# A new hand-written order of steps: the first loads move between two issuing queues, and a weight's last rows are loaded later

## The chip, the cores and the metric

The kernel runs on one core of one Trainium2 chip. The metric is device time in microseconds of one execution. Times are medians of several runs; the profile is of one further execution.

## The reference

One token sequence x of 2048 rows by 448 columns is normalised once, and the result feeds two branches, whose outputs are added to x.

```python
xn  = layernorm(x)                                  # over the 448 columns
q, k, v = split_heads(xn @ wqkv)                    # 16 heads of 28
phi(t) = concat(softmax(t @ w_phi), softmax(-(t @ w_phi)))      # per head, 56 features
kv  = einsum("sf,sd->fd", phi(k), v);  z = phi(k).sum(s)
o   = (phi(q) @ kv) / (phi(q) @ z + 1e-6)
h   = xn @ w1 + b1                                  # 1792 columns
out = x + o @ wo + (h * tanh(softplus(h))) @ w2
```

All tensors are bfloat16.

## The kernel before, in words

The 2048 rows lie as 16 tiles of 128 rows; two tiles make a *pair* u (tiles 2u and 2u+1), eight pairs in all. The program is a list of named steps. A string, `ORDER` (line 147), names them one after the other; `run_order` calls each, and a step appends its instructions to the queues of the engines that do it. Every engine (PE, DVE, ACT, POOL) and SP, which only issues transfers, then works through its own queue in that order. Waits between engines are derived from what a step reads and writes. So the string sets, for each engine, what stands behind what; a step that waits holds up all that follows on its engine. ACT issues a few transfers too, from the same queue as its arithmetic.

The steps that matter here:

- `lx1`, `lx2`, `lx3` load one pair of x each (line 270; "first pair" in the order of use is pair 3, tiles 6 and 7), `lx6`, `lx0`, `lx4` the rest. The last letter is the issuer: s for SP, a for ACT. `lp` loads w_phi (298), `lb` the bias (302).
- `lkm`, `lvm` load rows 0 to 383 of the K and V columns of wqkv into Wk and Wv (273); `lkt` loads the last 64 rows of both, twice, into the two halves of the partitions (281, the *tails*). `l1m0` to `l1m2` and `l1t` do the same for W1 (277, 281). `lqT0` to `lqT3` load the transposed Q columns (285). `l2s`, `los` load W2 and Wo.
- `z12` is twelve warm-up products of constants on PE. `wtk0` to `wtk3` transpose Wk on PE (556), `wmk`, `wmq` multiply Wk and WqT by the block-diagonal phi matrix that POOL builds (`bd`, 544); this folds phi into the projections Wpk and Wpq. Of these names the last letter is the engine that copies the result out of PSUM (a: ACT, d: DVE).
- Per pair: `st` statistics of a tile (467), `rs` the inverse deviation (on ACT or POOL), `xn` the normalised tiles (501 on DVE, 496 on POOL), `xt` the transpose into xnT: on PE with a copy (509; a, d, or b for half on ACT and half on DVE), or by a transfer (m, 521).
- `v`, `k`, `q` with a pair's number and part 1 or 2 are the projections of that pair (438; eight and six products). ACT takes the exponents of k and q; `kn` divides by their sums (608 to 612); `e` followed by a tile's number transposes a tile's exponents of q by a transfer (669).
- `f` is the first layer of the second branch with W1 (438, with 512 columns), `kv` sums phi(k) times v (629), `nd` is the attention's quotient (703 to 729), `wo`, `G`, `g` are the output products (805 to 843), and `sto` the stores.

Each part of six products waits for the end of its part of eight, and results leave PSUM through four pairs of banks. The transposing transfers of xn and of the exponents, the plain loads and SP's waits all share SP's one queue.

Of the kernel before, what the change touches and what calls it, by code (L numbers as in the profile page):

```python
# [144 lines left out]


ORDER = """
lpa pp2 lx3s pm z12 st6d pi lkms table st7d pw lx1a lkts lba lvma bd rs3t wtk2a xn3d lx2s lqT2 wtk0d st3d pv wtk1a wmk2a
xt3a wtk3d lqT1 wmk0a wmk1a st2d wmk3a st5d v31d rs1p lqT0 st4d xn1d rs2p lqT3 b1 qd lx6s v32a k31 lx0s wmq1a lx4s pp1
wmq0a xn2p l1ts xt1d st14d st15d wmq2a wmq3a k32 k11 st12d rs7p st9d q11 xt2m st8d k12 st10d xn7d q31 rs4p v11d pp0 q12  # L150
xn4p st11d v12d q21 rs5p st13d q32 q22 xn5p k21 st0d l1m2s l1m0s rs6p xt7m v21d k22 st1d v22a ep e3 rs0p v71a pk xt4m
k71 v72a kn3.1 xn6d k72 xt5m k41 xn0d kn3.0 e2 xt6m xt0m v41d e5 k42 l1m1s v42d e4 q41 v51d q42 e6 e8 v52a kn2.0 k61
v61d k62 kn4.0 k01 k51 kn7.0 kn4.1 k02 v62d q51 k52 q52 kn0.0 e7 q61 e9 v01d q62 e12 kn1.1 kn6.1 e10 f0.11 e11 kn1.0
v02d f0.12 kn0.1 f1.01 f0.21 f1.02 f1.21 kn7.1 f1.31 f1.22 los kn2.1 q71 f1.32 f1.51 kn5.0 f0.22 e13 f1.52 q01 q72 q02
f0.61 l2s kn6.0 kv3 kv1 e15 kv2 kn5.1 kv4 kv6 e14 kv7 kv0 kv5 kvz f0.62 f0.71 f0.91 f1.81 f0.72 e1 f1.82 f0.121 f1.111
f0.122 f0.81 f0.92 f1.112 f0.82 f1.91 f0.131 f1.92 e0 nd2 f0.132 f0.31 f0.101 f0.32 nd0 f0.111 f0.102 f0.112 nd1 f1.71
f1.61 f1.72 f0.51 nd3 f1.62 f0.52 f1.41 f1.11 f0.01 f1.12 f0.41 f1.42 ot0m nd5 f0.42 f0.02 wo01 f1.131 f1.101 ot1m nd6
f1.132 G01 nd4 f1.102 G11 ot2m wob nd7 ot3m G02 wo02 f1.121 nd12 G12 f1.122 wo11 nd11 wo22 G31 wo31 nd10 wo12 G21 nd13
ot5m ot6m wo21 wo32 G62 nd8 G22 wo52 G32 nd9 ot4m wo61 G51 nd15 G61 nd14 wo51 G41 wo62 sto6 sto1 wo41 G52 ot7m g14 sto5
wo7F sto2 G42 wo7H sto0 wo42 g15 stt14 sto3 sto4 stt15  # L160
"""


# [824 lines left out]
```

## Time and profile before

| | us |
|---|---|
| runs before the change | 150.36, 150.85, 152.3; median 150.85 |
| the profiled execution | 150.35, of which the span is 148.3 |
| PE busy | 143.7 (97% of the span) |
| DVE, ACT, POOL busy | 100.7, 72.0, 44.4 |
| granted PE clock | 0.999 |

The span runs from the first instruction to the last. A row of the timeline gives the start, the time from the first instruction of a group to the end of the last, the engine, the line and operation, what is written from what is read, and how many instructions are merged; behind it, in brackets, how long the engine was idle before and what ended that. SPq and ACTq rows are the issuing of transfers, not their flight. A row of the windows view gives the stretch and its length, then the busy time and count of instructions of PE, PE's weight loads, DVE, ACT and POOL, then the granted clock, the mean busy share of the 16 DMA engines, and GB/s. A row on DMA issues ends with the KB of each transfer and the median time from issue to landing.

### The profile page before, as it was taken

How to read it: one execution, taken by the hardware profiler on the slowest of the kernel's cores; microseconds unless marked ns; L12 is line 12 of the kernel's file. 1: busy time of each engine (PE TensorE's matmuls, PEld its weight loads, DVE VectorE, ACT ScalarE, POOL GpSimd, SP SyncE). 2: the span in 40 equal slices, each digit the busy share in tenths (PEclk: the TensorE clock that was granted, in tenths of full speed). 3: DMA queues.
4: the chain of work that ended last, by engine and by line, in shares of the span. 5: the costliest groups of instructions: out<-in, count | busy, mean ns of one | idle time of the engine just before them, and what ended most of it. 6: DMA issues, size and time to landing. Idle time of an engine off the chain costs nothing.

```text
span 148.3 us, 3988 instructions
## 1 busy us (share of the span) xinstructions
PE 143.7 (97%) x1731; PEld 75.9 (51%) x1731; DVE 100.7 (68%) x225; ACT 72.0 (49%) x83; POOL 44.4 (30%) x65
## 2 busy tenths in 40 slices
PE   7799999999999999999999999999999999999993
PEld 2456456556555475444454445555555555554452
DVE  0888889897999803003998278896789859983042
ACT  3589889978996899578566653202000000000000
POOL 5428489899899990000000000000000000000000
PEclk9999999999999999999999999999999999999999
DMA  5999998999939989960003300031003300306513
GB/s 123 301 190 346 182 275 130 163 205 256 139 67 174 242 242 267 210 113 0 0 4 62 62 4 0 21 73 34 4 2 66 62 0 4 62 4 186 186 52 134
DMA packets 39997, 17.24 MB, mean 116 GB/s; under 512 B 33964, under 2 KB 39212, under 8 KB 39980
## 3 DMA queue, kind: packets, MB, share of 16 engines
q1 hardware_dynamic: 38800, 16.29, 52.5%
q10 hardware_dynamic: 1180, 0.70, 1.9%
q8 instruction: 13, 0.21, 0.6%
q14 instruction: 4, 0.03, 0.1%
HBM read 7.02 MB, written 1.84 MB: 60 GB/s over the span
## 4 chain that ended last, share of the span: by engine, by line
PE 89%; DMA 6%; DVE 2%; issue 0%; ACT 0%; SPq 0%
PE PS L438 47%; PE PS L843 31%; PE PS L805 3%; DMA Wkv<-in_A_wqkv_dram 3%; DMA xnT<-xn 3%; PE PS L703 2%; PE PS L629 2%; PE PS L571 1%; PE PS L821 1%; DVE stats L467 1%; PE PS L556 1%; PE PS L509 1%; DVE xnT L516 0%; ACT Eq L514 0%; DVE x_all L770 0%
## 5 line engine op out<-in xcount | busy, mean ns | idle before, releaser
L438 PE MATMUL PS<-xnT,W 64*128 64x512 bf16 x392 | 44.8, 376 | 0.0
L680 ACT ACTIVATE actT<-PS,b1T 128x1024 bf16<-128x1024 f32 x28 | 30.1, 1112 | 24.3 <-PE PS L438 24.3
L843 PE MATMUL PS<-W,actT 64*128 64x448 bf16 x392 | 39.3, 349 | 0.0
L438 PEld LDWEIGHTS PS<-xnT,W 64*128 64x128 bf16 x392 | 18.8, 94 | 20.8 <-ACT actT L680 0.5
L843 PEld LDWEIGHTS PS<-W,actT 64*128 64x128 bf16 x392 | 18.1, 94 | 18.1 <-issue 0.3
L612 POOL TENSOR_TENSOR actT<-actT,rSk 128x896 bf16<-128x896 bf16 x16 | 26.6, 1702 | 0.7 <-DVE rSk L610 0.6
L770 DVE TENSOR_TENSOR x_all<-PS,x_all 128x448 bf16<-128x448 f32 (+1 forms) x16 | 9.2, 616 | 11.3 <-PE PS L821 5.6
L718 DVE COPY Sq<-PS 128x16 f32<-128x16 f32 x32 | 4.1, 169 | 18.6 <-PE PS L703 18.5
L608 DVE TENSOR_REDUCE Sk<-actT 128x32 f32<-128x896 bf16 x16 | 16.7, 1043 | 0.0
L600 ACT ACTIVATE actT<-PS 128x896 bf16<-128x896 f32 x16 | 13.8, 950 | 1.0 <-PE PS L438 0.9
L438 PE MATMUL PS<-Wkv,xnT 64*128 64x448 bf16 x112 | 13.2, 349 | 0.0
L438 PE MATMUL PS<-Wpq,xnT 64*128 64x448 bf16 x112 | 12.5, 349 | 0.4 <-DMA xnT<-xn 0.4
L467 DVE BATCH_NORM_STATS2 stats<-x_all 128x6 f32<-128x448 bf16 x16 | 9.7, 608 | 4.1 <-DMA x_all<-in_A_x_dram 4.1
L438 PE MATMUL PS<-Wpk,xnT 64*128 64x448 bf16 x112 | 12.5, 349 | 0.0
L726 DVE TENSOR_TENSOR v_all<-v_all 128x464 f32<-128x464 f32 x16 | 10.3, 642 | 0.6
L722 DVE TENSOR_TENSOR v_all<-PS,Sq 128x464 f32<-128x464 f32 x16 | 10.3, 642 | 0.5
L729 DVE TENSOR_TENSOR xn<-v_all,rden 128x448 bf16<-128x448 f32 x16 | 10.0, 625 | 0.6
L724 DVE TENSOR_TENSOR v_all<-PS,Sq 128x464 f32<-128x464 f32 x16 | 10.1, 631 | 0.0
L661 ACT ACTIVATE actT<-PS 128x896 bf16<-128x896 f32 x10 | 8.6, 921 | 1.1 <-PE PS L438 1.1
L438 PEld LDWEIGHTS PS<-Wpq,xnT 64*128 64x128 bf16 x112 | 5.9, 94 | 5.4 <-issue 0.8
L438 PEld LDWEIGHTS PS<-Wpk,xnT 64*128 64x128 bf16 x112 | 6.0, 94 | 4.4
L438 PEld LDWEIGHTS PS<-Wkv,xnT 64*128 64x128 bf16 x112 | 6.0, 94 | 4.3
(82 smaller groups left out, 126.4 us busy)
## 6 DMA issues: line engine op xcount, KB each, us to landing
W<-in_B_w_dram SPq DMA_DIRECT2D x1, 1568.0 KB, 10.1
out_dram<-x_all SPq DMA_DIRECT2D x7, 224.0 KB, 2.1
W<-in_B_w_dram SPq DMA_DIRECT2D x3, 448.0 KB, 4.1
x_all<-in_A_x_dram SPq DMA_DIRECT2D x2, 448.0 KB, 4.9
x_all<-in_A_x_dram SPq DMA_DIRECT2D x3, 224.0 KB, 3.8
Wo<-in_A_wo_dram SPq DMA_DIRECT2D x2, 336.0 KB, 4.1
W<-in_B_w_dram SPq DMA_DIRECT2D x2, 224.0 KB, 6.4
Wkv<-in_A_wqkv_dram SPq DMA_DIRECT2D x1, 336.0 KB, 4.5
```

Of the source, the lines that this page charges most:

```text
L438: ins = e.matmul(o, lhs(c, k), rhs(c, k), start=part == "1" and c == 0, stop=part == "2" and c == 2)
L467: op("DVE", lambda e: e.bn_stats(stats[:, t, :], x_all[:, t, :]), r=[("x", t)], w=[("st", t)], tag=f"bn{t}")
L600: op("ACT", lambda e, s=s: e.activation(E_of(u)[:, s, :, :], two(b, D), ACT.Exp, scale=1.0 if s == 0 else -1.0), r=[pb(b), pb(b + 1)], w=[ ...
L608: op("DVE", lambda e: e.tensor_reduce(Sk[u][:, s, :], Eh(), AX.X, ALU.add), r=[("E", u, s)], w=[("Sk", u, s)], tag=f"Sk{u}.{s}")
L612: op("POOL", lambda e: e.tensor_tensor(Eh(), Eh(), ap_on(rSk[u][:, s, 0:1], [[1, 2 * H], [0, DH]]), ALU.mult), r=[("E", u, s), ("rSk", u, ...
L680: op("ACT", lambda e: e.activation(actT[:, fc, q * 1024:(q + 1) * 1024], bank(b, 2), ACT.Mish, bias=b1T[:, fc:fc + 1]), r=[("b1T",), pb(b) ...
L722: op("DVE", lambda e: e.tensor_tensor(tv(t1[i]), num(0), sx(1), ALU.mult), r=[pb(b), pb(b + 1), ("Sq", i, 1)], w=[("t1", i)], tag=f"ta{t}")
L724: op("DVE", lambda e: e.tensor_tensor(tv(t2), num(1), sx(0), ALU.mult), r=[pb(b), pb(b + 1), ("Sq", i, 0)], w=[("t2",)], tag=f"tb{t}")
L726: op("DVE", lambda e: e.tensor_tensor(t1[i], t1[i], t2, ALU.add), r=[("t1", i), ("t2",)], w=[("t1", i)], tag=f"tc{t}")
L729: op("DVE", lambda e: e.tensor_tensor(o_sb[(t // 2) % 2][:, t % 2, :].rearrange("p (h d) -> p h d", d=DH), t1[i][:, :, 0:DH], ap_on(rden[i ...
L770: op("DVE", lambda e: e.tensor_tensor(x_all[:, t, 0:n], bank(b)[:, 0:n], x_all[:, t, 0:n], ALU.add), r=[pb(b), ("x", t)], w=[("out", t)], ...
L843: ins = e.matmul(bank(places[par][0])[:, 0:D], l, r, start=fresh[par], stop=places[par][2] and i >= len(todo) - 2)
```

## The change

Only the string `ORDER` differs; no step is added, and the functions stay as they are. Its beginning, before and after:

```diff
-lpa pp2 lx3s pm z12 st6d pi lkms table st7d pw lx1a lkts lba lvma bd rs3t wtk2a xn3d lx2s lqT2 wtk0d st3d pv wtk1a wmk2a
-xt3a wtk3d lqT1 wmk0a wmk1a st2d wmk3a st5d v31d rs1p lqT0 st4d xn1d rs2p lqT3 b1 qd lx6s v32a k31 lx0s wmq1a lx4s pp1
...
+pv z12 pi pm lx3a pp2 lba ep pk st6d pp0 lkms lkta lps st7d table lx1s lvma rs3t wtk2d lx2s pw b1 xn3d wtk1a wtk0d lqT0
+st3d wtk3a bd xt3b wmk2a st2d lqT1 wmk1a lqT3 rs1p st5d lqT2 st4d wmk3a xn1d wmk0a v31d lx6s v32a k31 wmq1a rs2p wmq2a
...
```

The rest of the string is permuted as well. All products stay; some copies change engine, pair 3's transpose is copied by ACT and DVE together (xt3b for xt3a), pair 0's inverse deviation is worked out by ACT instead of POOL, and pair 6 instead of pair 4 is normalised on POOL.

The first place is the head of the program, where ACT and SP issue the first loads. ACT before and ACT after (Wraw is w_phi, b_rows the bias; Wkv 64x896 the tails of Wk and Wv, Wkv 128x3x448 the main part of Wv here and of Wk on SP):

```order
L298 DMA Wraw<-in_A_w_phi_dram 112x4x28
L315 ACT_TABLE_LOAD
L270 DMA x_all<-in_A_x_dram 128x896
L302 DMA b_rows<-in_B_b_dram 14x128
L273 DMA Wkv<-in_A_wqkv_dram 128x3x448
```

```order
L270 DMA x_all<-in_A_x_dram 128x896
L302 DMA b_rows<-in_B_b_dram 14x128
L281 DMA Wkv<-in_A_wqkv_dram 64x896 x2
L315 ACT_TABLE_LOAD
L273 DMA Wkv<-in_A_wqkv_dram 128x3x448
```

ACT's x load was pair 1 and is pair 3 now; the tails came to ACT, and w_phi left it. SP in the same place, before and after:

```order
L270 DMA x_all<-in_A_x_dram 128x896
L273 DMA Wkv<-in_A_wqkv_dram 128x3x448
L281 DMA Wkv<-in_A_wqkv_dram 64x896 x2
L270 DMA x_all<-in_A_x_dram 128x896
L285 DMA_TRANSPOSE WqT<-in_A_wqkv_dram 128x448 x4
```

```order
L273 DMA Wkv<-in_A_wqkv_dram 128x3x448
L298 DMA Wraw<-in_A_w_phi_dram 112x4x28
L270 DMA x_all<-in_A_x_dram 128x896 x2
L285 DMA_TRANSPOSE WqT<-in_A_wqkv_dram 128x448 x4
L270 DMA x_all<-in_A_x_dram 128x1792
```

SP's x loads were pairs 3 and 2 and are pairs 1 and 2; the main part of Wk moved to the front.

The second place is DVE from its first statistics to the first token product, v31. Before, with the rows for pair 3 (tiles 6, 7) first, Eq being where transposes of Wk are copied to:

```order
L468 BN_AGGR mv<-stats 128x2
L467 BN_STATS stats<-x_all 128x6
L468 BN_AGGR mv<-stats 128x2
L501 TENSOR_SCALAR xn<-x_all,mv,rstd 128x448
L501 TENSOR_SCALAR xn<-x_all,mv,rstd 128x64
L501 TENSOR_SCALAR xn<-x_all,mv,rstd 128x384
L516 COPY Eq<-PS 112x512
L467 BN_STATS stats<-x_all 128x6
```

After, from the same place on:

```order
L468 BN_AGGR mv<-stats 128x2
L516 COPY Eq<-PS 112x512
L516 CAST b1T<-PS 128x14
L501 TENSOR_SCALAR xn<-x_all,mv,rstd 128x448
L501 TENSOR_SCALAR xn<-x_all,mv,rstd 128x64
L501 TENSOR_SCALAR xn<-x_all,mv,rstd 128x384
L516 COPY Eq<-PS 112x512
L467 BN_STATS stats<-x_all 128x6
L468 BN_AGGR mv<-stats 128x2
L516 COPY xnT<-PS 128x512
```

A copy and the bias's cast moved ahead of pair 3's normalisation, and the copy of half of the transposed pair 3 stands behind the statistics of tile 3, which is in pair 1.

The third place is SP behind the last load of x, before and after (W 64x1792 are W1's tails, W 128x1792 its chunks; xnT is the transpose of a pair, EqT that of a tile's exponents):

```order
L281 DMA W<-in_B_w_dram 64x1792 x2
L521 DMA_TRANSPOSE xnT<-xn 128x7x128
L277 DMA W<-in_B_w_dram 128x1792 x2
L521 DMA_TRANSPOSE xnT<-xn 128x7x128
L669 DMA_TRANSPOSE EqT<-actT 128x8x128
L521 DMA_TRANSPOSE xnT<-xn 128x7x128 x2
L669 DMA_TRANSPOSE EqT<-actT 128x8x128
L521 DMA_TRANSPOSE xnT<-xn 128x7x128 x2
L669 DMA_TRANSPOSE EqT<-actT 128x8x128
L277 DMA W<-in_B_w_dram 128x1792
```

```order
L277 DMA W<-in_B_w_dram 128x1792
L521 DMA_TRANSPOSE xnT<-xn 128x7x128
L669 DMA_TRANSPOSE EqT<-actT 128x8x128
L669 DMA_TRANSPOSE EqT<-Eq 128x8x128
L521 DMA_TRANSPOSE xnT<-xn 128x7x128
L277 DMA W<-in_B_w_dram 128x1792
L521 DMA_TRANSPOSE xnT<-xn 128x7x128
L669 DMA_TRANSPOSE EqT<-actT 128x8x128 x3
L521 DMA_TRANSPOSE xnT<-xn 128x7x128 x2
L669 DMA_TRANSPOSE EqT<-Eq 128x8x128
L281 DMA W<-in_B_w_dram 64x1792 x2
```

The second list begins behind the first chunk of W1 and the first transpose of a pair. W1's tails moved from the head of this stretch to its end, and its last chunk moved forward in front of three pairs' transposes.

More of the change, by code (lines that the diff above doesn't have):

```diff
@@ L147 @@
 ORDER = """
-lpa pp2 lx3s pm z12 st6d pi lkms table st7d pw lx1a lkts lba lvma bd rs3t wtk2a xn3d lx2s lqT2 wtk0d st3d pv wtk1a wmk2a
-xt3a wtk3d lqT1 wmk0a wmk1a st2d wmk3a st5d v31d rs1p lqT0 st4d xn1d rs2p lqT3 b1 qd lx6s v32a k31 lx0s wmq1a lx4s pp1
-wmq0a xn2p l1ts xt1d st14d st15d wmq2a wmq3a k32 k11 st12d rs7p st9d q11 xt2m st8d k12 st10d xn7d q31 rs4p v11d pp0 q12
-xn4p st11d v12d q21 rs5p st13d q32 q22 xn5p k21 st0d l1m2s l1m0s rs6p xt7m v21d k22 st1d v22a ep e3 rs0p v71a pk xt4m
-k71 v72a kn3.1 xn6d k72 xt5m k41 xn0d kn3.0 e2 xt6m xt0m v41d e5 k42 l1m1s v42d e4 q41 v51d q42 e6 e8 v52a kn2.0 k61
@@ L153 @@
[L153 to L157, printed above, removed]
@@ L158 @@
-f1.132 G01 nd4 f1.102 G11 ot2m wob nd7 ot3m G02 wo02 f1.121 nd12 G12 f1.122 wo11 nd11 wo22 G31 wo31 nd10 wo12 G21 nd13
-ot5m ot6m wo21 wo32 G62 nd8 G22 wo52 G32 nd9 ot4m wo61 G51 nd15 G61 nd14 wo51 G41 wo62 sto6 sto1 wo41 G52 ot7m g14 sto5
-wo7F sto2 G42 wo7H sto0 wo42 g15 stt14 sto3 sto4 stt15
+pv z12 pi pm lx3a pp2 lba ep pk st6d pp0 lkms lkta lps st7d table lx1s lvma rs3t wtk2d lx2s pw b1 xn3d wtk1a wtk0d lqT0
+st3d wtk3a bd xt3b wmk2a st2d lqT1 wmk1a lqT3 rs1p st5d lqT2 st4d wmk3a xn1d wmk0a v31d lx6s v32a k31 wmq1a rs2p wmq2a
@@ new lines @@
+wmq0a qd xn2p lx0s xt1d pp1 wmq3a lx4s st15d k32 st14d st11d v11a rs7p q11 v12a st8d q12 xn7d l1m0s q31 xt2m l1m2s xt7m
+e2 st9d k11 st10d st12d rs4p q32 k12 xn4d q21 rs5p xn5p e7 st0d v21d st1d xt4m kn1.1 k21 l1m1s v22a q22 v71a st13d k71
+v72d rs0a k72 xt5m xn0d rs6p k22 e3 e5 e4 v41d xn6p kn3.0 k41 v42d xt6m k42 kn7.1 q41 q51 xt0m q42 kn7.0 q52 v51d k51
+v52a kn4.0 k52 k61 v61d k62 kn2.0 kn3.1 v62d q61 e6 kn1.0 v01d q62 l1ts e9 kn2.1 v02d k01 f0.11 k02 e10 kn5.1 f0.21
+f0.12 kn6.0 f1.31 f1.51 f1.32 kn5.0 kn0.1 e11 f0.22 kn4.1 kn0.0 f1.21 f1.52 e13 q71 f1.01 f1.22 q01 f1.02 e8 e12 f0.61
@@ new lines @@
+q72 l2s kn6.1 q02 e0 kv4 kv1 kv5 kv7 kv0 kv3 e15 kv2 kv6 f0.62 f1.81 f1.71 kvz f1.82 f1.72 f0.31 los e1 f0.121 f0.51
+f0.32 f0.91 f0.122 nd2 f0.92 f0.52 f1.61 f0.101 f1.62 f0.71 nd3 f0.102 f1.111 f0.72 e14 f1.112 ot1m nd1 f0.01 f1.11
+f0.02 nd6 f0.41 f1.12 wob f0.81 f0.42 f1.41 nd7 f0.82 f0.131 f1.42 nd0 f0.111 f0.132 ot3m ot0m f0.112 f1.101 nd5 f1.131
+f1.102 f1.132 f1.121 nd4 G01 f1.91 ot2m wo01 f1.122 nd10 G02 wo11 wo02 f1.92 nd12 G12 nd13 nd11 G11 G61 ot6m wo31 sto0
+G31 wo61 wo32 ot5m nd8 wo12 G62 nd15 wo62 G32 sto3 sto6 nd14 ot7m G21 wo21 nd9 wo51 wo22 ot4m G22 g14 wo7F G51 wo41 wo52
@@ L161 @@
+G41 sto2 G52 wo7H sto1 G42 sto5 wo42 stt14 sto4 g15 stt15
 """
```

## The prediction

> **What bounds the kernel now.** First the page's busy row, then the windows on both sides of the last wait that PE shows, then the end of the chain that ended last.
>
> ```profile
> span 148.3 us, 3988 instructions
> PE 143.7 (97%) x1731; PEld 75.9 (51%) x1731; DVE 100.7 (68%) x225; ACT 72.0 (49%) x83; POOL 44.4 (30%) x65
> 18.64:145.36 126.72, 126.72 (x1567) 66.89 (x1568) 87.11 (x186) 58.89 (x61) 34.98 (x37) 1.00 0.50 101
> 0.85:18.64 17.79, 16.50 (x153) 8.63 (x154) 12.82 (x39) 13.06 (x23) 9.21 (x25) 1.00 0.98 240
> 142.96 2.40 PE PS L805 x14
> 145.38 0.56 DVE x_all L770
> ```
>
> From 18.64 to 145.36 us PE is busy in all of its 126.72 us. Ahead of that it is idle for 17.79 - 16.50 = 1.29 us, while the DMA engines are busy 0.98 of the time. After 145.36 come the last addition and the last store, 148.3 - 145.4 = 2.9 us, whose steps stand last in both orders. So all that an order can win is those 1.29 us, 0.9% of the time; what it can lose is any new wait of PE. Two per cent, 3.0 us, is about what a measurement of this kernel can tell from no change, and it is more than twice what is there to win.
>
> Where the idle time lies:
>
> ```profile
> 0.85 4.65 PE L376 MATMUL PS<-const-bfloat16-1.0 128*128 128x512 bf16 x12 [0.85 <-PEq L973]
> 5.94 0.85 PE L556 MATMUL PS<-ident,Wkv 128*112 128x128 bf16 x12 [0.44 <-DMA Wkv<-in_A_wqkv_dram]
> 7.12 0.36 PE L571 MATMUL PS<-Wbd,Eq 112*128 112x112 bf16 x4 [0.33 <-ACT Eq L514]
> 7.81 0.43 PE L556 MATMUL PS<-ident,Wkv 128*112 128x128 bf16 x4
> 9.06 0.93 PE L438 MATMUL PS<-Wkv,xnT 64*128 64x448 bf16 x8
> 18.64 2.07 PE L438 MATMUL PS<-Wpq,xnT 64*128 64x448 bf16 x20 [0.40 <-DMA xnT<-xn]
> ```
>
> The warm-up (z12) ends at 0.85 + 4.65 = 5.50; Wk's main part lands 0.44 later; the first product with phi waits 0.33 for the copy of a transpose; the first token product (v31) begins at 9.06; and q21 waits 0.40 for the transposed third pair xnT 2.
>
> **The start, part by part.** The change reorders the first loads of two queues. What each load took:
>
> ```profile
> 0.81 0.39 SPq L270 DMA_DIRECT2D x_all<-in_A_x_dram  x1
> 1.26 0.42 SPq L273 DMA_DIRECT2D Wkv<-in_A_wqkv_dram  x1
> 1.73 1.19 SPq L281 DMA_DIRECT2D Wkv<-in_A_wqkv_dram  x2
> 1.30 0.48 ACTq L270 DMA_DIRECT2D x_all<-in_A_x_dram  x1
> x_all<-in_A_x_dram ACTq DMA_DIRECT2D x1, 224.0 KB, 4.1
> Wkv<-in_A_wqkv_dram SPq DMA_DIRECT2D x2, 112.0 KB, 5.1
> Wkv<-in_A_wqkv_dram ACTq DMA_DIRECT2D x1, 336.0 KB, 5.2
> Wraw<-in_A_w_phi_dram ACTq DMA_DIRECT2D x1, 24.5 KB, 3.0
> 2.00:4.00 2.00, 2.00 (x6) 0.76 (x5) 0.36 (x1) 0.55 (x1) 0.80 (x4) 1.00 1.01 271
> 4.00:6.00 2.00, 1.56 (x6) 0.48 (x5) 1.79 (x6) 1.00 (x4) 1.54 (x3) 1.00 1.08 288
> ```
>
> Both queues draw on one stream of some 280 KB/us from about 2.0 us, and I let them share it evenly. In the trace SP's second tail and ACT's Wv both land at about 7.7 us, which fits. Landing is put 0.7 us behind the last byte. By that:
>
> - *Wk* goes first on SP, at 0.81. It and ACT's x pair 3 run side by side: pair 3 (224 KB) lands at 2.0 + 448/280 + 0.7 = 4.3 (3.6 before), Wk at 2.0 + 672/280 + 0.7 = 5.1 at the latest, under the warm-up. The 0.44 us wait goes.
> - *The tails of Wk and Wv* are on ACT behind pair 3 and land near 6; the transposes that need them come fourth, at about 6.3 (7.81 before).
> - *Pair 3's normalisation* sets the next bound, by these rows of the timeline and the chain:
>
> ```profile
> 3.64 0.63 DVE L467 BATCH_NORM_STATS2 stats<-x_all 128x6 f32<-128x448 bf16 x1 [3.64 <-DMA x_all<-in_A_x_dram]
> 5.17 1.23 DVE L501 TENSOR_SCALAR xn<-x_all,mv,rstd 128x448 bf16<-128x448 bf16 x3
> 6.38 0.61 ACT Eq L514
> 6.60 0.42 DVE L516 COPY Eq<-PS 112x512 bf16<-112x512 bf16 x1 [0.21 <-PE PS L556]
> 7.48 0.39 PE PS L509 x7
> 10.83 0.86 DVE L501 TENSOR_SCALAR xn<-x_all,mv,rstd 128x448 bf16<-128x448 bf16 x3
> 11.56 0.50 PE PS L571 x8
> 11.60 0.17 DVE L516 CAST b1T<-PS 128x14 f32<-128x14 bf16 x1
> ```
>
> Its statistics took from 3.64 to the normalisation's 5.17, 1.5 us, and start 0.7 later, so they are through at 5.9. Now the copy of a transpose (0.42) and the bias's cast (0.17) also stand ahead of it on DVE. The first transpose takes 0.85/3 = 0.28 and its copy came 0.16 behind that (6.38 - 5.94 - 0.28): the copy runs from 5.50 + 0.44 = 5.94 to 6.36, the cast to 6.5, the normalisation (0.86, as at 10.83; its first tile can start then) to 7.3. PE idles from 6.65 to 7.3, transposes (0.39) and makes four products of 0.25: v31 could begin at 8.7.
>
> *Pair 1 of x* decides whether it does. It leaves ACT for SP, behind Wk and phi. On DVE st3, the statistics of pair 1's second tile, now stand in front of the copy of the transposed pair 3's second half (the second place shown under the change), and v31 cannot start without that copy. So v31 now waits for pair 1's load too; before, ACT made the whole of the copy. Ahead of pair 1's last byte SP moves 336 + 24.5 + 224 KB and ACT as much, 1169 KB, 4.2 us; phi's small pieces I price at 0.8 us more, between nothing and its whole 3.0 us to landing, nearer the small end because it ran beside 224 KB of x in those 3.0 us. That gives 2.0 + 4.2 + 0.8 + 0.7 = 7.7; with statistics of 0.63, a gap of 0.1 for their end and a copy like the 0.42 above, with 0.15 for two hand-overs, v31 begins at 9.0, against 9.06. Ends: 5.4, where it landed before (then v31 at 8.7), and 8.7. From 7.4 on, every microsecond that pair 1 is late costs one.
>
> The Trainium skill, "DMA: Bandwidth & Descriptors", section "Issuing engines are not separate DMA queues", says that DMAs of all issuing engines run on the same 16 engines and interleave, so that spreading them saves only the time of issuing. It speaks against the change: pair 3's move to ACT buys Wk 0.45 us, and pair 1 pays. The common landing at 7.7 agrees; were the queues independent, pair 1 would land near 5 and v31 would begin at 8.7.
>
> **From v31 to q21.** PE went from 9.06 to 18.24 without a real gap, 9.18 us. The bias's transpose (0.11) is now in front; v32 follows v31 directly and waits about 0.1 for its end, so these cancel. One part of six products (q32, 0.57) moves ahead of q21. PE arrives at 9.0 + 9.18 + 0.57 = 18.75. The third pair's transpose was issued at 14.22 and took 4.29:
>
> ```profile
> 14.22 4.29 DMA xnT<-xn
> xnT<-xn SPq DMA_TRANSPOSE x6, 3.5
> 3.60 5.12 SPq L285 DMA_TRANSPOSE WqT<-in_A_wqkv_dram  x4
> WqT<-in_A_wqkv_dram SPq DMA_TRANSPOSE x4, 4.1
> ```
>
> Its statistics hang on the same DVE and POOL chain, which starts about 0.2 later; the chunk of W1 issued ahead of it has the same 448 KB as the two tails had. So it lands at 14.4 + 4.3 = 18.7, and q21 begins at 18.85. Before, at that point of the work, it was 18.64 + 0.57 = 19.21. **Gain: 0.36 us.** The products of Wq come in between, at 9.0 + 2.2 = 11.2 behind v31, v32 and k31. The last of the four WqT transposes, issued at 3.60 + 5.12 - 1.28 = 7.4 before, goes out at 6.8 now and lands at 10.9 by the median of 4.1. I count no wait; a microsecond more would cost 0.7.
>
> **What comes later.** Two waits have little slack. One is for xT4, the fifth pair's transpose: SP now issues two transposes of exponents (eT2, eT7) ahead of it, where it was one. It goes out three issues of 1.32 behind xT7, at 22.2, lands 3.5 later at 25.7, and PE needs it 6.65 us behind q21 (five parts of eight products at 0.76, five of six at 0.57), at 25.5. I charge 0.2 for it, between nothing and the 1.0 that a landing as slow as xT2's 4.29 would cost.
>
> W1's tails went out next to the loads of x and now follow e6, the second transposed tile of pair 3.
>
> ```profile
> W<-in_B_w_dram SPq DMA_DIRECT2D x2, 224.0 KB, 6.4
> W<-in_B_w_dram SPq DMA_DIRECT2D x3, 448.0 KB, 4.1
> 18.92 1.23 SPq L521 DMA_TRANSPOSE xnT<-xn  x1
> 29.47 1.31 SPq L669 DMA_TRANSPOSE EqT<-actT  x1
> 36.06 2.37 SPq L669 DMA_TRANSPOSE EqT<-Eq  x1
> 39.83 1.04 PE L438 MATMUL PS<-xnT,W 64*128 64x512 bf16 x8
> ```
>
> xT7 went out at 18.92; DVE has one pair of statistics (0.7) less between rs7 and its normalisation now, so 18.2. From there SP issues 11 transposes at 1.32 with their gaps and one chunk at 0.6: the tails go out at 33.3 and 33.9, up to 1.06 later where an issue is stretched as at 36.06. They land 4.1 to 6.4 later, the second one at 38.0 to 41.3. The first product with W1 (f0.11) has 43 parts of v, k and q ahead of it in both orders, so it is due at 39.83 - 0.36 = 39.5. I take 4.8, nearer the 4.1 of the chunks that were issued after x was in; so 38.7, and no wait. The cover is 0.8 us.
>
> **Sum.** The profiled execution took 150.35 us, 148.3 of span and 2.05 around it. 150.35 - 0.36 + 0.2 = **150.2 us**. It lies at the bottom of the runs before (150.36 to 152.3, median 150.85), so a median of runs may come out above it.
>
> **Rivals.**
>
> 1. *Pair 1 lands late, slower.* Place: st3 in front of the copy for v31 on DVE. Past 7.9 the net gain of 0.16 is used up; at the upper end, 8.7, the time is 150.2 + 1.0 = 151.2. For it: a DMA share of 1.08 from 4 to 6 us. Against: pair 1 is only third in SP's queue. Chance 0.15.
> 2. *W1's tails land late.* Past 39.5 f0.11 waits; a landing 6.4 behind its issue costs 0.8, with the stretched issue 1.8, and the middle, 1.3, gives 151.5. For it: the 6.4 of these same loads. Against: that was in the rush of x, and chunks later took 4.1. Chance 0.2.
> 3. *The change does not do what it says:* Wk is early, but pair 3's normalisation and xT2 give it back, and PE ends where it did: 150.4, with up to 0.3 of small waits. Chance 0.15.
> 4. *All goes well:* pair 1 by 7.4 and xT2 in its median 3.5, so that v31 begins at 8.7 and q21 at 18.45, 0.76 earlier, no wait at xT4: 149.6. Chance 0.15.
>
> The forecast, 149.9 to 150.6, has 0.35. The range reaches from 149.3 (case 4 with 0.3 us of scatter) to 151.6 (case 2's end). Slower by over 2% would need two late loads together, more than 3 us: 0.03. Faster by over 2% is barred by the 1.29 us of idle time, but for the scatter of the runs: 0.02.
>
> **What would show it.** In the changed profile: no wait of PE for Wkv at 5.5, an idle stretch of about 0.65 us in front of PE's transposes of xn near 7.3, v31 near 9.0 and, just ahead, DVE's copy into xnT behind a wait for x_all; q21 near 18.85; PE without a gap from then on, but for up to 0.4 at the first Wkv product near 25.5. Wrong would be: v31 past 9.5, PE waiting for W at 39 to 41, or PE waiting for exponents between 30 and 36, where ACT is nearly full.

## The result, and the profile after

The changed kernel takes 152.51 us (median of 22 runs), the kernel before 150.73 us (22 runs beside them); the ratio is **1.0093 [1.0066, 1.012]**. It is about 1% slower, where a time within the runs of before was predicted (150.2 us). Ratios leave out the runs of a kernel that lie more than 1.5% above its fastest (four of these 22, and one of e9_sp_order at 702.83 us), so they need not be the quotients of the medians, which are of all runs. The profiled execution took 152.76 us with a span of 151.0, against 150.35 and 148.3. The page and the windows by stage, which answer to those of before:

```profile
span 151.0 us, 3987 instructions
PE 144.4 (96%) x1731; PEld 76.5 (51%) x1731; DVE 99.9 (66%) x226; ACT 72.0 (48%) x85; POOL 43.3 (29%) x63
0.85:18.64 17.79, 16.11 (x143) 8.61 (x145) 12.17 (x40) 11.47 (x21) 9.85 (x29) 1.00 0.92 226
30.00:60.00 30.00, 28.45 (x380) 17.05 (x378) 21.36 (x33) 24.88 (x28) 24.69 (x16) 1.00 0.88 177
60.00:148.00 88.00, 88.00 (x1083) 44.55 (x1078) 55.15 (x128) 24.76 (x23) 0.23 (x1) 1.00 0.34 65
```

PE still has no gap from 60 to 148 us. It is idle for 17.79 - 16.11 = 1.68 us in the head (1.29 before) and for 1.55 between 30 and 60, where there was no idle time before. PE's timeline shows the three waits, with the places that were to gain:

```profile
0.84 5.28 PE L376 MATMUL PS<-const-bfloat16-1.0 128*128 128x512 bf16 x12 [0.84 <-PEq L973]
8.33 0.43 PE L556 MATMUL PS<-ident,Wkv 128*112 128x128 bf16 x4 [1.08 <-DMA Wkv<-in_A_wqkv_dram]
10.55 1.74 PE L438 MATMUL PS<-Wkv,xnT 64*128 64x448 bf16 x14 [0.54 <-DMA Wkv<-in_A_wqkv_dram]
20.15 0.92 PE L438 MATMUL PS<-Wpq,xnT 64*128 64x448 bf16 x8
31.90 2.07 PE L438 MATMUL PS<-Wpq,xnT 64*128 64x448 bf16 x20 [1.55 <-DMA xnT<-xn]
42.49 1.04 PE L438 MATMUL PS<-xnT,W 64*128 64x512 bf16 x8
```

The last transpose of Wk waits 1.08 us for its tail, v31 waits 0.54 for Wv and begins at 10.55 instead of 9.06, q21 (20.15) waits for nothing, q51 waits 1.55 for xT5, and f0.11 begins at 42.49 instead of 39.83. (xT with a pair's number is the transposing transfer of that pair, eT with a tile's number that of the tile's exponents.) By its parts that is +1.49 at v31, -0.40 for xT2's wait, +1.55 at q51: 2.64, against 2.66 measured at f0.11 and 2.7 in the span. The time grew by 2.41 only, since 1.76 us lie outside the span instead of 2.05. Of the 2.66, idle time is 1.92; the other 0.74 is busy time, for the same 378 products ahead of f0.11 took 38.42 us instead of 37.68, 0.63 of it in the warm-up (5.28 against 4.65). The longer warm-up did not set v31, which began 0.14 behind Wv's landing: in e1_chunk_late below it took 4.10, and v31 still began at 10.50. The chain that ended last names the two transfers, and the list of DMA issues shows the first loads (KB of each, median us to landing):

```profile
3.20 7.21 DMA Wkv<-in_A_wqkv_dram
24.81 6.95 DMA xnT<-xn
x_all<-in_A_x_dram ACTq DMA_DIRECT2D x1, 224.0 KB, 3.2
Wkv<-in_A_wqkv_dram SPq DMA_DIRECT2D x1, 336.0 KB, 4.4
Wkv<-in_A_wqkv_dram ACTq DMA_DIRECT2D x2, 112.0 KB, 5.4
Wkv<-in_A_wqkv_dram ACTq DMA_DIRECT2D x1, 336.0 KB, 7.2
```

Wk lands at 0.8 + 4.4 = 5.2, under the warm-up. Wv on ACT, issued at 3.20 (2.50 before), lands at 10.4 (7.7 before), and the tails, issued at 1.97 and 2.53, at 6.95 and 8.28 (6.49 and 7.77 before).

### The profile page after: what moved, and what is told of

Read it like the earlier page. It is cut to its first block, busy times and chain, and to the rows that moved or that the text cites. A ratio compares the mean times of both kernels' runs of the same rounds, so it can differ in the third digit from the quotient of the medians.

```text
span 151.0 us, 3987 instructions
## 1 busy us (share of the span) xinstructions
PE 144.4 (96%) x1731; PEld 76.5 (51%) x1731; DVE 99.9 (66%) x226; ACT 72.0 (48%) x85; POOL 43.3 (29%) x63
## 4 chain that ended last, share of the span: by engine, by line
PE 79%; DMA 9%; DVE 6%; ACTq 1%; SPq 1%; issue 1%; ACT 0%
PE PS L438 39%; PE PS L843 31%; DMA Wkv<-in_A_wqkv_dram 5%; DMA xnT<-xn 5%; PE PS L805 3%; DVE stats L467 3%; PE PS L703 2%; PE PS L629 2%; DVE mv L468 1%; DVE xn L501 1%; PE PS L821 1%; ACTq L281 1%; SPq L521 1%; PE PS L571 0%; ACTq L302 0%
## 5 line engine op out<-in xcount | busy, mean ns | idle before, releaser
L843 PEld LDWEIGHTS PS<-W,actT 64*128 64x128 bf16 x392 | 18.6, 94 | 17.2 <-issue 0.3
L438 PE MATMUL PS<-Wpk,xnT 64*128 64x448 bf16 x112 | 13.0, 349 | 0.0
```

The source lines that it names most:

```text
L438: ins = e.matmul(o, lhs(c, k), rhs(c, k), start=part == "1" and c == 0, stop=part == "2" and c == 2)
L843: ins = e.matmul(bank(places[par][0])[:, 0:D], l, r, start=fresh[par], stop=places[par][2] and i >= len(todo) - 2)
```

## The experiments

All ratios are to the kernel before, run beside. Theory A: the tails and Wv are late because they share ACT's queue with pair 3. Theory B: W1's second chunk in front of xT5 makes it late. Rival C: the order of copies, statistics and transposes costs. Theory D, made on the way: reads of PE's instructions hold up the transfer they fall on.

### One part undone, one part alone

**e1_chunk_late**, the changed kernel:

```diff
-... rs0a k72 xt5m ... k21 l1m1s v22a ...
+... q41 q51 xt0m l1m1s q42 ...
```

> The changed kernel with one load moved back: the last chunk of W1 is issued behind xT0 instead of in front of xT5. Theory B (the chunk delays the fifth pair's transpose, 1.55 us of PE wait in the changed profile): that wait is gone, and the kernel is 0.7 to 1.5 us faster than the changed one, ratio to before 1.000 to 1.005; v31 still begins near 10.5. Theory A (the late tails and Wv on ACT's queue carry the loss): the wait may go, but the ratio stays at 1.007 to 1.011. Rival C (the new order of copies and statistics on DVE and ACT): no change, 1.009.

**e2_old_head**, the changed kernel with the loads of before:

```diff
-lx3a lba lkms lkta lps table lx1s lvma
+lx3s lpa lkms table lx1a lkts lba lvma
```

> The changed kernel with the first loads of SP and ACT as they were before (pair 3, Wk, the tails and pair 2 on SP; w_phi, pair 1, the bias and Wv on ACT); all else as changed. Theory A: v31 begins at 9.0 +- 0.3 instead of 10.55, and the ratio to before falls to 0.996 to 1.003. Theory B alone: v31 comes earlier, but the wait for xT5 grows by as much, ratio 1.007 to 1.010. Rival C: v31 stays past 10 us, for the bias and the copies stand in front of pair 3's normalisation on DVE.

**e3_both** has both edits.

> The changed kernel with both moved back: the first loads as before, and the last chunk of W1 behind xT0. If A and B together are the loss: v31 near 9.0, no wait of PE at q51, and 0.3 to 0.6 us faster than before (ratio 0.996 to 0.999), since the wait for xT2 at q21 is gone. Rival C: still slower than before, 1.004 or more.

**e4_chunk_early**, the kernel before with the chunk in front of xT5:

```diff
-k72 xt5m k41 ... k42 l1m1s v42d
+k72 l1m1s xt5m k41 ... k42 v42d
```

> The kernel before with one load moved: the last chunk of W1 in front of xT5, as the change has it. Theory B: PE waits 1 to 2 us for xT5 at v51, ratio to before 1.005 to 1.012. If a chunk in front of a transpose is harmless by itself and only met a busy queue in the changed kernel: 1.000 to 1.002 and xT5 lands in 3.5 to 4.5 us.

**e5_new_head**, the kernel before with the changed loads: the reverse of e2's edit.

> The kernel before with only the first loads in the changed order (pair 3, bias and tails on ACT; Wk, phi, pair 1 on SP); everything from the first statistics on stands as before. Theory A (tails and Wv are late on ACT's queue): the last transpose of Wk waits for its tail to about 8.3, v31 begins at 10.0 to 10.6 instead of 9.06, part of it is won back at xT2, ratio 1.004 to 1.009. Rival C (the head's order of copies and statistics in the changed kernel costs, not the loads): v31 at 9.3 or earlier, ratio 1.000 to 1.003.

| | ratio | waits of PE over 0.3 us behind the warm-up, in order of time |
|---|---|---|
| e1_chunk_late (clock 0.989) | 1.0124 [1.0078, 1.017] | tails 2.01, v31 0.49, f0.11 1.24 |
| e2_old_head | 1.0102 [1.0064, 1.0139] | tails 0.87, xT5 1.53, f0.11 0.71 |
| e3_both | 1.0076 [1.0046, 1.0106] | tails 0.51, ACT's copy 0.39, xT4 1.10 |
| e4_chunk_early | 1.0048 [1.0022, 1.0075] | Wk 0.57, phi 0.33, xT5 1.20 |
| e5_new_head | 1.0050 [1.0023, 1.0078] | phi 0.85, tails 0.54, v31 0.91 |

A and B are each confirmed as a cost by itself: put alone into the kernel before they make 0.5% each, with the waits that they name. (e5 also waits 0.85 for the phi matrix, since phi goes to SP with the changed loads; but v31 is set by Wv, which lands at 10.55.) The timelines of e5 and e4:

```profile
8.45 0.43 PE L556 MATMUL PS<-ident,Wkv 128*112 128x128 bf16 x4 [0.54 <-DMA Wkv<-in_A_wqkv_dram]
10.68 0.93 PE L438 MATMUL PS<-Wkv,xnT 64*128 64x448 bf16 x8 [0.91 <-DMA Wkv<-in_A_wqkv_dram]
```

```profile
30.67 0.93 PE L438 MATMUL PS<-Wkv,xnT 64*128 64x448 bf16 x8 [1.20 <-DMA xnT<-xn]
```

In e5's profile v31 comes 1.62 us late and f0.11 1.06 (40.89 against 39.83), since xT2 no longer makes PE wait; the medians differ by 0.65 us (151.08 against 150.43).

Taken out of the changed kernel, neither gave its part back: e1, e2 and e3 all lie above the ratios that A and B expected (the intervals of e1 and e2 reach into the upper ones), and e3's 0.76% is what rival C expected. In e1 and e2 the wait that was aimed at went or shrank (no wait at q51; v31 at 9.59), but PE then stood before f0.11:

```profile
43.63 1.04 PE L438 MATMUL PS<-xnT,W 64*128 64x512 bf16 x8 [1.24 <-DVE rSk L610]
42.44 1.04 PE L438 MATMUL PS<-xnT,W 64*128 64x512 bf16 x8 [0.71 <-DVE rSk L610]
```

The view names DVE, whose instruction had ended 0.8 and 0.3 us earlier. What landed just ahead is the second of W1's tails, at 43.55 in e1 and 42.35 in e2, 0.08 and 0.09 before f0.11. In the changed kernel itself it landed at 42.21, and f0.11 began at 42.49 without a wait. So tails of W1 that land there would hold f0.11 to about where the two other losses put it; no run moved them alone. In e3 they landed at 40.77, before f0.11 (41.50), and what is left is a wait of 1.10 for xT4 and two smaller ones. (The waits for Wk's tail in e2 and e3 are not a late load: it lands at 7.93 and 7.73, against 7.77 before; the changed order brings PE to that transpose earlier.) Waits here do not add up. A PE that is late early on finds later transfers landed.

### Theory D: the reads of instructions

In the changed kernel's trace xT5 is in flight from 24.81 to 31.76. Half a microsecond there, and what followed, in the view of windows (the last two columns are the DMA share and GB/s), and the one packet of the instruction queue that moved from 28.0 to 28.5:

```profile
28.00:28.50 0.50, 0.50 (x10) 0.22 (x8) 0.50 (x1) 0.50 (x2) 0.50 (x1) 1.00 2.91 114
28.50:30.00 1.50, 1.50 (x20) 0.76 (x16) 1.47 (x3) 1.50 (x3) 1.50 (x4) 1.00 0.11 9
q8 instruction: 1, 0.02, 11.7%
```

A 16 KB packet comes, and for 1.5 us almost nothing moves (9 GB/s), with xT5, the chunk and a transpose of exponents outstanding. To move these reads, the next two kernels make the warm-up of 80 narrow products.

**e6_after_phase** (the changed kernel) and **e8_before_phase** (the kernel before):

```diff
-for _ in range(n):  ... bank(b)[:, :], ..., [0, TCW]
+for _ in range(80): ... bank(b)[:, :64], ..., [0, 64]
```

> The changed kernel with the warm-up as 80 products of 64 columns instead of 12 of 512 (its result is not used). That is 68 products more, so the 16 KB reads of PE's instructions, one per some 120 products, come at other points of the work: the second one near 20 us instead of 28.4, the third near 32. Theory D (a transposing transfer that is in flight at such a read is held up by 1.5 to 2 us): xT5, issued near 24.8, lands after 4 to 5 us instead of 7.0, q51 waits under 0.4 instead of 1.55, and the ratio is 1.1% (of 1.55 us) or so under that of the changed kernel, near 1.000, unless another transpose is hit at 20 or 32. Rival B (W1's chunk in front of xT5 alone makes it late): q51 still waits 1.2 to 1.6, ratio 1.007 to 1.012.

> The kernel before with the warm-up as 80 products of 64 columns instead of 12 of 512 (its result is not used), so that the reads of PE's instructions come some 68 products earlier in the work: the first near 9, the second near 19 instead of 24.6, the third near 30 instead of 36.7. Theory D: xT2 (issued near 14.2) is free of a read and lands after 3.0 to 3.5 us instead of 4.3, so q21's wait of 0.40 goes; a transpose in flight near 19 or 30 takes 5 us or more, and PE waits for it if it has under 1.5 us of slack; ratio 0.995 to 1.006. Without D: xT2 takes 4.3 as before and the wait stays; ratio within 0.3% of 1, but for the warm-up's own length.

The page's row of the instruction queue, before and in e6:

```profile
q8 instruction: 13, 0.21, 0.6%
```

```profile
q8 instruction: 14, 0.23, 0.7%
```

68 more products bring one packet more, as they would if the queue is PE's. The first three packets came near 9.5, 17.5 and 31.5 us in e6 instead of 15.5, 28.5 and 40, and near 9.5, 20.5 and 30.5 in e8 instead of 15.5, 24.5 and 37. The landings of the transposed pairs, of the changed kernel and of e6:

```profile
DMA to landing us min/median/max: 3.0/3.2/7.0
```

```profile
DMA to landing us min/median/max: 3.0/3.6/5.2
```

In e6 the longest, xT5's, fell to 5.2 us and q51's wait for it went (0.39 for ACT is left); in e8 q21's wait went, though there v31 is 0.90 late as well (9.96). Both waits as D expected. A packet alone is not enough, however: in the changed kernel xT2 was in flight from 15.03 to 18.25 when one came at 15.43, and landed after 3.22 us. The ratios do not bear D out: 1.0145 [1.0096, 1.0194] and 1.0052 [1.0016, 1.0087]. The granted clock was 0.978 to 0.989 in four of e6's six runs (below), but the two at full clock took 151.65 and 152.23 us; that is not 1.55 less than the 152.08 of the changed kernel at full clock. Of e8's twelve runs ten had the full clock, five from 150.20 to 151.11 us and five from 152.21 to 152.76; the profile is of one of the first five, and what the others lose is not known.

**e11_filler** was made for the clock and bears on theory D as well:

```diff
-pv z12 pi
+pv z18 pi
```

> The changed kernel with 18 products in the warm-up instead of 12 (the six more run into the time in which PE waits for the tails). Theory F: an idle stretch of PE of 1 to 2 us near 7 can drop the granted clock to a half for some 3.4 us, as in the profiled execution of e1_chunk_late; with PE busy there the clock stays at 1.00 in all runs, and the time is that of the changed kernel's undisturbed runs, ratio 1.007 to 1.011, since the tails, Wv and xT5 stay as late as they were. Rival: PE's idle time ahead of the tails is not idle in effect (its six transposes then come late): v31 over 10.8, ratio 1.012 or more.

The order on SP is that of the changed kernel, with the chunk in front of xT5. In the profiled execution the packet came at 24.6, 0.4 us behind the issue of xT5, no stall followed, and the same stretch went on at 181 GB/s:

```profile
28.50:30.00 1.50, 1.50 (x20) 0.80 (x16) 1.50 (x3) 1.50 (x3) 1.50 (x2) 1.00 1.22 181
30.00:32.00 2.00, 2.00 (x26) 0.99 (x24) 1.93 (x4) 1.71 (x3) 1.69 (x2) 1.00 1.07 213
```

PE waits for no transpose, and the span is 148.8. Sorted over all profiles, one for each kernel, xT5 took from issue to landing (a stall is at least 1 us under 40 GB/s within its flight):

| us | no stall | a stall |
|---|---|---|
| W1's chunk right ahead of it | 5.05 (e11), 5.23 (e6) | 6.95 (changed), 6.90 (e2), 6.66 (e4) |
| no chunk right ahead | 4.32 (before), 3.89 (e8), 4.50 (e13) | 4.49 to 5.34 (nine kernels) |

So chunk and stall each go with a later landing, and only where both met did PE wait for xT5. A packet of the instruction queue came right ahead of the stall in the changed kernel and in e4, and 2.5 us ahead of it in e2. Over its runs e11 scatters from 150.56 to 153.28, ratio 1.0105 [1.0066, 1.0144], so the runs that were not profiled mostly lost more than this one, and their traces were not kept. That the packet causes the stall is not shown, only that in these profiles the two mostly go together.

### SP's order of transposes

**e7_uncrowded** and **e9_sp_order** start from e3; SP's transposes of exponents eT2 and eT7 go behind xT5, in e7 with a transpose of Wk later on PE, in e9 with W1's tails early. **e10_splice** has the order of before on every engine up to k31, then the changed one with eT2, eT7 and the chunk late.

```diff
 e3:  xt7m e2 ... e7 ... xt4m ... xt5m
+e7:  xt7m ... xt4m ... xt5m e2 e7;  wmk2a wtk3a
+e9:  l1ts xt2m ... xt7m ... xt4m ... xt5m e2 e7
+e10: (before, to k31 ... xt1d) then xt7m ... xt4m ... xt5m e2 e7
```

> The changed kernel with the first loads as before, W1's second chunk behind xT0, the transposes of exponents eT2 and eT7 behind xT4 and xT5, and the last transpose of Wk behind four products with phi as before. If the loss is A plus B plus a third part (a transpose that stands too early on PE, and transposes of exponents ahead of xT4): v31 at 9.0 to 9.2, no wait for xT4 or xT5 over 0.3, ratio 0.996 to 1.001. If the third part lies elsewhere in the new order (copies on other engines): no wait at these places, but others behind 30 us, ratio 1.003 to 1.008. By theory D a read of instructions can still hit xT4 or xT5, with a wait up to 0.7.

> The run e3_both (the changed kernel with the first loads as before and W1's second chunk behind xT0) with two more steps of SP where they were: the transposes of exponents eT2 and eT7 behind xT4 and xT5, and W1's tails ahead of xT2. If what e3_both still lost (0.76%, a wait of 1.10 us for xT4) comes from the transposes of exponents in front of xT4: no wait for xT4 or xT5 over 0.3, f0.11 without a wait, v31 near 9.4 as in e3_both, ratio 0.998 to 1.003. If the loss lies in the order on PE, DVE and ACT: other waits take its place, ratio 1.004 to 1.009.

> Every engine in the order of before up to the first product with WqT of pair 1's turn (behind v31, v32 and k31), then the order of the changed kernel, with eT2, eT7 and W1's second chunk behind xT5 and xT0. If the rest of the new order costs nothing by itself: v31 at 9.0 to 9.3, ratio 0.997 to 1.002, and e9_sp_order is slower than this by what its v31 is late (0.3 us, 0.2%). If the order of projections and copies after the head costs: waits of PE between 12 and 45 us, ratio 1.004 or more.

All three missed their first theory: 1.0252 [1.0217, 1.0287], 1.0072 [1.0047, 1.0097], 1.0105 [1.0067, 1.0143]. e9 and e10 lie in the range of their second theory, but the wait is for a transfer of SP's. xT4 and xT5 are in time in all of them, and the wait has moved on to xT6 (1.02, 0.77 and 1.64 us, the last of them in e10's timeline here); e7 waits besides 0.88 for a copy on ACT that my edit put late, and 1.89 for W1's tails:

```profile
35.99 0.93 PE L438 MATMUL PS<-Wpk,xnT 64*128 64x448 bf16 x8 [1.64 <-DMA xnT<-xn]
```

```profile
44.02 1.04 PE L438 MATMUL PS<-xnT,W 64*128 64x512 bf16 x8 [1.89 <-DMA W<-in_B_w_dram]
```

**e12_crowd** is the kernel before with one transpose moved:

```diff
-pk xt4m ... kn3.0 e2 xt6m
+pk e2 xt4m ... kn3.0 xt6m
```

> The kernel before with one transpose of exponents, eT2, moved from behind xT5 to ahead of xT4; nothing else. If SP's queue is what sets xT4 and xT5: xT4 and xT5 go out 1.3 us later, xT4 near 22.9; with a landing 3.0 to 4.9 us behind the issue it is there at 25.9 to 27.8, against 25.9 when k41 needs it: a wait of 0 to 1.9 us, most likely 0.5 to 1.0, ratio 1.002 to 1.008. If the transposes have slack: no wait, ratio within 0.2% of 1.

It costs 1.0129 [1.008, 1.0178], more than expected. xT4 goes out at 23.08 instead of 21.55 and takes 4.74, with a packet of the instruction queue at 25.5 and a stall from 26 to 27; e3's xT4 took 4.87 across such a stall too, the changed kernel's 3.03 without one:

```profile
27.96 0.93 PE L438 MATMUL PS<-Wpk,xnT 64*128 64x448 bf16 x8 [1.78 <-DMA xnT<-xn]
```

**e13_splice_sp** and **e14_sp_as_before** move three transposes of exponents of e10 and e9 behind xT6 and xT0:

```diff
-xt5m e2 e7 ... e3 e5 e4 ... xt6m ... xt0m
+xt5m e2 e7 ... xt6m ... xt0m e3 e5 e4
```

> e10_splice with the transposes of exponents eT3, eT5 and eT4 behind xT6 and xT0 instead of ahead of them; nothing else. If SP's order is the last part: xT6 goes out near 29.6, when POOL has normalised pair 6, instead of 32.66, and lands before the 34.3 at which PE wants it; the wait of 1.64 us goes, ratio 0.999 to 1.004 (the 0.50 for xT2 stays). If the order on the other engines costs: the wait turns up at another place, ratio 1.006 or more.

> e9_sp_order with eT3, eT5 and eT4 behind xT6 and xT0; so SP's loads and transposes stand as before in all places that were named, with the changed order on PE, DVE, ACT and POOL. If SP's order is the last part: no wait for xT6 (0.77 in e9_sp_order), v31 at 9.4 to 9.8, ratio 1.000 to 1.004. If the other engines' order costs: ratio 1.006 or more with waits at other places.

The second theory's sign came true, a wait at another place, but neither foresaw the size: 1.0487 [1.0448, 1.0526] and 1.052 [1.0481, 1.0559]. xT6 was in time, but ACT stood still for 4.50 us (4.30 in e14), and PE behind it. The view names no cause for ACT's wait; its next exponents of q began at 35.54, 0.07 behind the landing of the first of the three transposes that had been moved (issued at 32.21, landed at 35.47), so I read it as waiting for a buffer of exponents. From e13's timeline:

```profile
32.21 4.07 SPq L669 DMA_TRANSPOSE EqT<-actT  x3
35.54 1.73 ACT L661 ACTIVATE actT<-PS 128x896 bf16<-128x896 f32 x2 [4.50 <-issue]
37.32 1.42 PE L438 MATMUL PS<-Wpk,xnT 64*128 64x448 bf16 x8 [2.80 <-ACT actT L661]
```

Part of the size is the clock: all twelve runs had a granted clock of 0.967 to 0.989, and in e13's profile it was 0.50 from 38 to 44 us. A mean of 0.978 over 156 us is up to 3.4 us of the 7.6 that this run lost.

So SP could not serve both in these runs. In the kernel before two transposes of exponents stand ahead of xT6, which goes out at 26.71; in the changed order there are five, and xT6 goes out at 32.58. Moving one transpose of exponents ahead of xT4 costs 1.3% by itself (e12), moving them behind xT4 and xT5 makes xT6 late (e7, e9, e10), and moving them behind xT6 holds up ACT. That what e3 still lost is this lack of slack on SP from xT4 to xT6 is argued from these runs; none of them took the loss away, and a cure without the old order of products was not tried.

### Wk first, tails on SP

**e15_wk_first**, the kernel before:

```diff
-lpa lx3s lkms table lx1a lkts lba lvma
+lx3a lpa lkms lkts table lx1s lba lvma
```

> The kernel before with pair 3 on ACT and Wk first on SP as in the changed kernel, but phi ahead of the bias on ACT behind pair 3, the tails on SP behind Wk, and pair 1 on SP behind them. By the shares seen (ACT's queue gets about a third of the stream): Wk lands at 5.2, the tails at 7.0 to 7.5, Wv on ACT near 8.3; PE has no wait for Wk (0.44 before), v31 begins at 8.7 to 9.2, ratio 0.996 to 1.002. If Wv on ACT is what sets v31: it lands after 9, v31 at 9.3 to 10, ratio 1.002 to 1.006.

1.0026 [1.0006, 1.0046], and v31 at 9.45: Wk still made PE wait 0.37 behind a warm-up of 4.39, phi landed later (a wait of 0.56 for its matrix), and a copy on DVE cost 0.36. With the tails on SP they land at 6.18 and 6.75, against 6.95 and 8.28 behind pair 3 on ACT in the changed kernel, which supports theory A. But Wv landed at 9.32 and not near 8.3, 0.13 before v31, so the second theory's place and ratio fit as well. No version beat the kernel before.

## Why the prediction was wrong, point by point

- *PE without slack, 1.29 us to win, any new wait to lose:* right in the main. All of the loss lies in front of f0.11, 1.92 of its 2.66 us as idle time; that the same warm-up products can take 0.63 longer was not in the sum.
- *Wk at 5.1, under the warm-up:* right, 5.2.
- *The tails near 6, Wv early enough:* **this step failed.** It rested on an even sharing of the stream, read from a common landing at 7.7. But by 7.7 SP had moved 224 + 336 + 224 = 784 KB and ACT 224 + 336 = 560 (phi's 24.5 left out), so ACT's share from 2.0 to 7.0 was 112 KB/us and not 140. In the changed kernel it was 784 KB from 2.0 to 9.7, 102 KB/us: about a third of the 280. ACT now had to bring 784 KB, and I had followed only its tails, by a rate too high; Wv's place behind the tails was not in the sum at all. Price: v31 at 10.55, not 9.0. Even the third is a mean: of ACT's loads pair 3 landed at 4.03, the two tails of 112 KB at 6.95 and 8.28, and Wv's 336 KB only 2.1 us behind them. That landing comes 0.7 behind the last byte was assumed; no row shows it.
- *The page's rule:* the Trainium skill, "DMA: Bandwidth & Descriptors", section "Queues, rings and completion order", says that a DMA engine takes turns between its queues by whole packets. It promises no even shares of bytes, and the 784 against 560 KB were not even. By ACT's 112 KB/us alone, without the page, Wv would have been put at 2.0 + 784/112 + 0.7 = 9.7, nearer to the 10.4 than any even share.
- *Pair 3's normalisation done at 7.3, pair 1 as the bound at 9.0:* the normalisation began at 7.08 instead of 6.5 and was done at 7.96, as the longer warm-up put the copy ahead of it off to 6.66; it was not the bound. Nor was pair 1, which landed at 6.18 and not 7.7: the even share erred here too, the other way. DVE reached st3 at 8.21 without a wait for x (rival 1 fell):

```profile
7.08 0.88 DVE L501 TENSOR_SCALAR xn<-x_all,mv,rstd 128x448 bf16<-128x448 bf16 x3
8.21 0.62 DVE L467 BATCH_NORM_STATS2 stats<-x_all 128x6 f32<-128x448 bf16 x1
9.19 0.42 DVE L516 COPY xnT<-PS 128x512 bf16<-128x512 bf16 x1
```

- *q21 without a wait:* the 0.40 went, at 20.15 instead of 18.85 because of the late v31. The landing was right by luck: xT2 went out at 15.03 and not 14.4, took 3.22 and not 4.3, and landed at 18.25, where 18.7 was reckoned.
- *0.2 for xT4, and no gap from then on:* **the second failed step.** xT4 caused no wait, since PE was 1.3 late. xT5 I had not looked at, though the chunk of 448 KB right ahead of it was in the counted order, and I had priced the transposes by their median of 3.5 with 4.29 as the worst; it took 6.95, which with a chunk ahead was seen only across a stall (the table under theory D). SP's queue:

```profile
22.82 1.33 SPq L521 DMA_TRANSPOSE xnT<-xn  x1
24.19 0.58 SPq L277 DMA_DIRECT2D W<-in_B_w_dram  x1
24.81 1.23 SPq L521 DMA_TRANSPOSE xnT<-xn  x1
26.08 6.46 SPq L669 DMA_TRANSPOSE EqT<-actT  x3
```

- *W1's tails, 38.7 and no wait:* **the third failed step**, hidden in the changed kernel. They were issued at 36.66 and 37.31 and not at 33.3 and 33.9, as SP's row of three above took 6.46 us where three times 1.32 was reckoned; with a landing 4.90 later, close to the 4.8 of the sum, the second was there at 42.21; f0.11 did not wait only because it was itself 2.66 late. In e1, e2 and e7 it waited 1.24, 0.71 and 1.89 and began 0.08 to 0.09 behind that landing. Rival 2's mechanism is real; its chance was too small, and it lies behind the other two losses.
- *Faster by 0.36 through xT2:* the wait that was to go went, and it was the least of the terms.

## What to carry to other kernels

Where one engine is full, follow every transfer that a changed queue carries to the instruction that needs it, with the rate of that queue alone (bytes by landing, per issuer), not an even share; the transfers behind the one that you look at pay for it. The waits of one engine for late transfers do not add up, so undo parts in both directions: a part that costs 0.5% alone may bring back nothing when it is taken out, where another late transfer stands right behind it. Transposes on one queue with a microsecond of slack should be priced by their worst landing in the trace, not by the median, and a move of buffers' readers earlier is also a demand on that queue.

## What the runs showed of the hardware

- Reads of PE's instructions (13 packets of 16 KB for 1731 products) mostly go along with stalls of the data stream of 1 to 1.5 us, at 9 GB/s in the rows above. The Trainium skill, "Runtime: NRT & Kernel Launch", section "Instruction fetch mechanics", has 16 KiB blocks of 256 instructions and calls the fetch hidden by the issue of instructions; the packets agree (1731 products and 1731 weight loads over 256 are 13.5), and no row here shows PE waiting for one, but the transposes in flight across a stall landed later.
- An idle stretch of PE in the head can cost the clock. In e1's profiled execution PE idled 2.01 us up to 8.32, and the granted clock (third column from the right) then fell:

```profile
10.00:11.00 1.00, 0.51 (x5) 0.34 (x6) 0.93 (x4) 1.00 (x4) 0.47 (x2) 0.70 1.28 305
11.00:12.00 1.00, 1.00 (x8) 0.18 (x3) 0.97 (x4) 0.50 (x2) 0.57 (x2) 0.50 0.99 353
12.00:13.00 1.00, 0.94 (x8) 0.32 (x8) 0.73 (x4) 0.00 (x0) 0.88 (x2) 0.50 1.04 393
13.00:14.00 1.00, 1.00 (x10) 0.45 (x8) 0.16 (x1) 0.42 (x1) 0.73 (x2) 0.59 1.07 423
14.00:15.00 1.00, 1.00 (x18) 0.63 (x15) 0.00 (x0) 0.66 (x2) 1.00 (x3) 1.00 0.78 305
```

  A half clock for (0.30 + 0.50 + 0.50 + 0.41) / 0.5 = 3.4 us costs 1.7 us, and a mean of 0.989 over 151 us is 1.7 us as well. In e13 the clock fell to 0.50 behind an idle stretch of 2.80 us; behind the changed kernel's 1.08 it did not fall. The Trainium skill, "TensorE: Matmul & The Clock Gate", Part 1, states half rate after an idle window of about 3.4 us and the full rate again after about 3.4 us of sustained work; the length of the drop in e1 agrees with the second, while the idle time ahead of it was shorter than the first. Five of the changed kernel's 22 runs had a mean clock of 0.988 or 0.989, against one of the 78 runs of the kernel before that were taken beside the experiments; with the gap cut to 0.68 (e11) none of eight had, which fits but is too few to settle it. The 17 runs at full clock have a median of 152.08 us, so most of the 1% does not come from this.
- The warm-up of the same twelve products took 4.06 to 5.28 us in the profiles. Whether Wk makes PE wait (0.44 before, 1.20 in e13) hangs on that as much as on the load.
